# An attention and SwiGLU kernel: ScalarE's instructions in one up phase keep the order in which the program writes them

## The chip, the cores and the metric

The kernel runs on one core of a Trainium2 chip. Such a core has a matrix engine (TensorE, PE in the profile), a vector engine (VectorE, DVE), a scalar engine (ScalarE, ACT) and a general engine (GpSimd, POOL), each with an instruction stream of its own. They read and write an on-chip memory of 128 partitions (SBUF); TensorE writes its results to a second one (PSUM), from which VectorE and ScalarE take them. Transfers to and from the chip's large memory, and here also between two places of SBUF, are issued from the queue of SyncE (SP) or of ScalarE. An engine takes up its instructions in the order of its stream; between engines, semaphores hold an instruction back until what it needs is there.

The metric is the device time of one execution in microseconds (us), the median of several. Lower is better.

## The reference

```python
def _attn_ref(q, k, v, g_norm):                      # q, k, v: (8, 8, 576, 64)
    kv = np.einsum('bhsd,bhse->bhde', k, v)
    out = np.einsum('bhsd,bhde->bhse', q, kv)
    rms = np.sqrt(np.mean(out * out, axis=-1, keepdims=True) + 1e-06)
    return (out / rms * g_norm).astype(np.float32)

def _moe_ref(x, w_gate, w_val, w_out):               # (4608, 512), (512, 1536) twice, (1536, 512)
    g = x @ w_gate
    silu = g * (1.0 / (1.0 + np.exp(-g)))
    val = x @ w_val
    return (silu * val @ w_out).astype(np.float32)
```

The first function is attention without a softmax: for each of 8 batches and 8 heads k-transposed times v gives a 64 x 64 matrix, q times that matrix gives the output, and each row of 64 is divided by its root mean square and multiplied by `g_norm`. The result, brought into the shape 4608 x 512, is the `x` of the second function, a feed-forward block with a SiLU gate. Inputs and outputs are float32 (the weights of the second function arrive as 64-bit words, which the kernel turns into float32 itself).

## The kernel before, in words

The 4608 rows are cut into nine blocks of 512. For each block there is an attention part (class `Att`), which makes the transposed activations `x`, and a feed-forward part (class `Ffn`), which has an up phase (the products with `w_gate` and `w_val`) and a down phase (the product with `w_out`). The large products are made by Strassen's scheme in Winograd's form: seven products of half-size matrices in place of eight, numbered 1 to 7, with sums of operands before them and sums of results after them. Blocks 0, 1 and 2 go alone (function `alone`), blocks 3 to 8 in pairs with two levels of the scheme. While block n computes, the attention part of later blocks is done between its steps.

**The up phase of block 2.** Method `Ffn.up` goes through six units, numbered 0 to 5 (class `Up`, one per 256 columns of the weights). The sequence of a unit's products is line 701: products 1 and 5 of this unit, 4 and 3 of the unit before, then 6, 2 and 7 of this one. After the last unit, `last.end()` (lines 733 to 737) makes its products 3 and 4. What is done with each product's result, by the unit's methods:

- after product 1, line 677: ScalarE copies bank `b` from PSUM to the tile piece `s`; after product 6, line 681: it copies bank `b` to `u2`; after product 7, line 711: it copies bank `b` to `u3`, and line 714 applies SiLU to `s`.
- after product 4, line 724: ScalarE applies SiLU to bank `b`, and line 725 has GpSimd multiply the result with `u3` into the hidden activations `h`.
- after product 2, line 707: VectorE adds bank `a` to `s`; after product 7, line 715: it adds bank `c` to `u3`; after product 3, line 728: it adds bank `c` to `u2`, and line 729 has GpSimd multiply it with `s` into `h`.
- The bank `b` runs on through products 1, 6, 7 and 4, so each of these waits for the copy after the one before it. The bank `c` runs on through products 5 and 3: product 3 of a unit accumulates onto `c`, and so waits for the VectorE add of line 715, which reads `c` after product 7.
- `h_sums` (lines 1080 to 1086) makes two VectorE sums for each unit, the owed ones of the unit before after line 715.

All simple VectorE and GpSimd operations are made through the helpers of lines 130 to 132, so the profile puts every add on line 130, every subtraction on line 131 and every multiplication on line 132; tile names tell them apart. The matmuls of the up and down phases are all on line 661.

**The attention work that is woven in.** Function `ahead` (lines 1253 to 1295) gives the up phase of block 2 a table of extra steps, keyed by unit and product. The keys that matter: at (4, 1) `place_x` (line 515) issues 16 transfers inside SBUF, line 522, all on SyncE's queue here, which bring the transposed activations of block 3 to their place in `arena`; at (4, 2) `raw` adds transfers that send weight pieces to memory (line 920); at (5, 5) `gain_x` (line 526) has ScalarE multiply these activations by `g_norm`, two instructions of 128 x 1024 elements on line 529, which need all 16 transfers; at (5, 6) `sums` appends the four VectorE sums of `sum_steps` (lines 536 to 542), which are then issued two at a time after the next products: s1 and s3 after product 2 of unit 5, the other two after product 7.

**What sets the order.** The kernel is written with a library that schedules: each engine's stream is arranged at build time by priority and by the scheduler's own estimate of when an instruction can start, and it may differ from the order in which the program writes the instructions. Two means bind it: `tc.issue_after(i)` puts what a block writes behind one instruction, and the context manager `in_order` (lines 135 to 150) ties each instruction written inside it to the one written before it on the same engine. It takes the engines as arguments. Around block 2, TensorE is in order as a whole (line 1366), and VectorE during the up phase (line 1341). ScalarE, GpSimd and SyncE are not. In the kernel before, the scheduler has put the two instructions of line 529 behind line 714 of unit 5, that is, behind the last SiLU that precedes the end of the up phase.

Of the kernel before, what the change touches and what calls it, by code (L numbers as in the profile page):

```python
# [18 lines left out]
def kernel(  # L19
# [41 lines left out]
    nc = tc.nc  # L61
# [72 lines left out]
    @contextmanager  # L134
    def in_order(*engines):

        traced = nc.cur_bb.bb.instructions
        last = traced[-1]
        yield
        start = next(k for k in reversed(range(len(traced))) if traced[k] is last) + 1  # L140
        before = {}
        for i in traced[start:]:
            if engines and i.engine not in engines:
                continue
            if i.engine in before:
                tc.add_manual_dep(
                    i, before[i.engine].name,
                    mybir.DependencyInfo(mybir.DependencyClass.NoSync, mybir.DependencyReason.DATA), reason="order",
                )
            before[i.engine] = i  # L150
# [1074 lines left out]
    def weights(upto):  # L1225
        nonlocal rounded
        while rounded < min(upto, len(pieces)):
            load_weights(rounded + 4)
            round_w(*pieces[rounded])
            rounded += 1  # L1230

    def t2(place, b22, b11):

        sub(nc.vector, place, b22, place)
        add(nc.vector, place, place, b11)
# [9 lines left out]
    def visit(ffn, att, gs, apart=False):  # L1245

        with tc.issue_after(ffn.multiplied.ins):
            for g in gs:
                att.kv(g, apart)
        if att.n < B:  # L1250
            ffn.visited = att.positions

    def ahead(ffn, att, then):

        def load(att, i):
            return lambda: ffn.sends.extend(att.quarter_steps(i, (0, 1), (nc.sync,)))

        def first():
            visit(ffn, att, (0, 1))
            ffn.sends += [load(att, 0), lambda: then.load_kv(0), load(att, 1)]  # L1260

        def turn(i):
            ffn.chores.append(lambda: att.turn_q(i))

        def second():
            visit(ffn, then, (0,), True)
            ffn.sends.append(lambda: then.load_kv(1))

        def half(i):
            with tc.issue_after(ffn.multiplied.ins):  # L1270
                att.heads(i, range(NS), (m_psum, m_psum))
            ffn.visited = att.multiplied
            ffn.chores += att.chores(i)
            if i:
                ffn.chores += att.turn_steps()

        def rest():
            for i in range(2):
                load(then, i)()

        def raw():
            for j in range(2, NP):
                ffn.sends += raw_steps(j)

        def sums():
            ffn.chores.extend(att.sum_steps())

        for j in (NP - 2, NP - 1):
            ffn.making.extend(kept_steps(j, chunks(h_alone[:, NF - 4 :]) if j == NP - 1 else chunks(xi_alone)))

        return {
            (0, 1): first, (1, 6): lambda: turn(0), (1, 7): second, (2, 1): lambda: half(0), (2, 6): lambda: turn(1),
            (2, 7): rest, (3, 1): lambda: half(1), (3, 7): lambda: visit(ffn, then, (1,), True), (4, 1): att.place_x,
            (4, 2): raw, (5, 5): att.gain_x, (5, 6): sums,
        }

    def alone(n):
        ffn = Ffn(n, blocks[n])
        nxt = blocks[n + 1]
        if n == 0:  # L1300

            with tc.issue_after(squared.ins), tc.issue_after(scaled.ins):
                weights(2)
            ffn.plain_up(0, (0,))
            copied = blocks[0].copied
            blocks[0].turn_x(1)
            for f in range(NF):
                with tc.issue_after(blocks[0].copied.ins if f else copied.ins):
                    weights(2 * (f + 2))
                ffn.plain_up(f) if f else ffn.plain_up(0, (1,))  # L1310
            weights(len(pieces))
            pairs = wo.rearrange("p (j e) d -> p e j d", e=2)
            t2(pairs[:, 0, :, HD:DM], pairs[:, 1, :, HD:DM], pairs[:, 0, :, 0:HD])
            nxt.room = xi_alone.rearrange("p a b c -> p (a b c)")

            with tc.issue_after(sent.ins):
                for i in range(2):
                    nxt.load_kv(i)
                for i in range(2):
                    nxt.load_q(i)  # L1320
            ffn.plain_end()
            for g in range(2):
                nxt.kv(g)
            nxt.turn()
        elif n == 1:

            def third():
                visit(ffn, nxt, (0,))
                nxt.load_kv(1)

            def two_thirds():
                visit(ffn, nxt, (1,))
                for i in range(2):
                    nxt.load_q(i)

            ffn.up({(1, 7): third, (3, 7): two_thirds})
            nxt.turn()
            for g in range(2):
                blocks[PAIRED].load_kv(g)
        else:  # L1340
            with in_order(nc.vector.engine):
                ffn.up(ahead(ffn, nxt, blocks[PAIRED + 1]))
            nxt = blocks[PAIRED + 1]
            nxt.turn()
            for g in range(2):
                blocks[PAIRED + 2].load_kv(g)
        if n == 2:
            ffn.down_.opens = PAIRED

        def inner_sums():  # L1350
            with tc.issue_after(nxt.scaled.ins):
                blocks[PAIRED].inner_sums()

        ffn.down(nxt, {7: inner_sums} if n == 2 else {})
        if n == 0:
            blocks[2].load_kv(0)

            with tc.issue_after(nxt.halves[0].ins):
                for j in range(NP // 2):
                    t2(wv[j][:, 0:2], wv[j][:, 2:4], wg[j][:, 0:2])  # L1360
            with tc.issue_after(ffn.down_.s4.ins):
                for j in range(NP // 2, NP):
                    t2(wv[j][:, 0:2], wv[j][:, 2:4], wg[j][:, 0:2])

    for n in range(PAIRED):
        with in_order(nc.tensor.engine) if n == 2 else ExitStack():
            alone(n)
# [61 lines left out]
```

## Time and profile before

| | us |
|---|---|
| median of three executions | 1023.85 (1022.38 to 1024.58) |
| the profiled execution's own time | 1026.13 |
| its span, first to last instruction | 1024.4 |
| TensorE busy with matmuls | 998.7 (97% of the span) |
| VectorE busy | 667.3 (65%) |
| ScalarE busy | 232.1 (23%) |
| GpSimd busy | 369.8 (36%) |

The profile comes from one execution. Its time lies 1.73 us above its span and 2.28 us above the median. Times inside it are counted from the span's start. A row of the timeline gives start, duration, engine, line, operation, output and inputs, and in brackets how long the engine had stood idle and what ended that. A matmul's end is modelled, so its duration overlaps that of the next one; the distance between starts is the pace. The up phase of block 2 ends, and its down phase begins, at about 361 us.

### The profile page before, as it was taken

Reading aid. Unit: us, or ns where it says so; the run is one execution under the profiler, and the core shown is the slowest. Engines: PE = TensorE matmul, PEld = TensorE weight load, DVE = VectorE, ACT = ScalarE, POOL = GpSimd, SP = SyncE. Lnnn points to the kernel's source line nnn. Section 1 sums busy time; section 2 is a strip of 40 time slices with the busy share of each in tenths; the row PEclk is TensorE's granted clock in tenths of the full one; section 3 lists DMA queues with packets and bytes.
Section 4 is the critical chain, followed back from the end, with each engine's and each line's share of the span. In section 5 each row is a group of like instructions: output and inputs, shape, how many; then the busy total and the mean of one; then the engine's idle time right before and its main releaser. Section 6 shows DMA issues by size and latency. Waiting matters only on the chain.

```text
span 1024.4 us, 17093 instructions
## 1 busy us (share of the span) xinstructions
PE 998.7 (97%) x6506; PEld 832.7 (81%) x6506; DVE 667.3 (65%) x1118; ACT 232.1 (23%) x367; POOL 369.8 (36%) x290
## 2 busy tenths in 40 slices
PE   5999999999999799999999999999999999999998
PEld 4544688888888688888888888888888888888887
DVE  2998897759767475666666846666767566666211
ACT  2765111221122212121111212112112121121100
POOL 0000363525444140454556003554650026546600
PEclk9999999999999899999999999999999999999999
DMA  7689643656566925676753265667321655553011
GB/s 218 200 266 251 118 88 134 217 165 147 165 140 113 227 58 162 167 208 164 169 144 51 89 159 152 160 173 179 101 34 50 144 160 146 150 145 95 1 42 42
DMA packets 254290, 143.23 MB, mean 140 GB/s; under 512 B 149504, under 2 KB 236544, under 8 KB 254208
## 3 DMA queue, kind: packets, MB, share of 16 engines
q1 hardware_dynamic: 223488, 138.20, 50.2%
q10 hardware_dynamic: 30656, 3.94, 2.4%
q8 instruction: 52, 0.85, 0.4%
q14 instruction: 30, 0.25, 0.1%
q0 software_dynamic: 64, 0.00, 0.0%
HBM read 104.99 MB, written 28.70 MB: 131 GB/s over the span
## 4 chain that ended last, share of the span: by engine, by line
PE 76%; DVE 9%; DMA 5%; SPq 5%; issue 2%; ACT 2%; POOL 1%; DVEq 0%; POOLq 0%; ACTq 0%
PE b L811 21%; PE b L661 21%; PE c L661 11%; PE c L811 10%; PE a L661 5%; PE a L811 5%; SPq L333 2%; DVE r L190 1%; PE m L431 1%; DMA ld<-in_moe_w_out_dram 1%; DVE arena L131 1%; PE m L370 1%; DVE arena L199 1%; SPq L522 1%; DMA ld<-in_v_dram 1%
## 5 line engine op out<-in xcount | busy, mean ns | idle before, releaser
L811 PE MATMUL b<-arena,t 128*128 128x256 f32 x1008 | 244.6, 381 | 0.0
L811 PEld LDWEIGHTS b<-arena,t 128*128 128x128 f32 x1008 | 189.9, 190 | 29.9 <-DVE r L130 2.8
L130 POOL TENSOR_TENSOR r<-r 128x256 f32<-128x256 f32 (+1 forms) x90 | 94.8, 1054 | 246.2 <-DMA t<-w 149.5
L130 DVE TENSOR_TENSOR r<-b,r 128x512 f32<-128x512 f32 (+1 forms) x234 | 139.0, 607 | 61.1 <-PE b L811 56.0
L130 DVE TENSOR_TENSOR r<-c,r 128x512 f32<-128x512 f32 (+1 forms) x170 | 104.7, 624 | 108.6 <-PE c L811 41.1
L131 POOL TENSOR_TENSOR t<-wo 128x512 f32<-128x512 f32 x54 | 78.1, 1468 | 175.9 <-DVE wo L130 107.2
L132 POOL TENSOR_TENSOR arena<-r 128x1024 f32<-128x1024 f32 (+1 forms) x54 | 100.9, 1883 | 112.3 <-DVE r L130 84.4
L130 DVE TENSOR_TENSOR r<-a,r 128x512 f32<-128x512 f32 x93 | 59.2, 637 | 110.5 <-PE a L661 73.6
L811 PE MATMUL c<-arena,t 128*128 128x256 f32 x504 | 122.5, 379 | 1.0 <-ACT r L825 0.8
L131 DVE TENSOR_TENSOR arena<-arena 128x512 f32<-128x512 f32 (+3 forms) x96 | 104.3, 1102 | 18.1 <-PE b L661 14.0
L811 PEld LDWEIGHTS c<-arena,t 128*128 128x128 f32 x504 | 95.6, 190 | 14.7 <-ACT r L825 1.2
L661 PE MATMUL b<-wo,arena 128*128 128x256 f32 x432 | 98.3, 382 | 0.4 <-issue 0.3
L661 PE MATMUL b<-t,arena 128*128 128x256 f32 x432 | 96.4, 379 | 1.4 <-POOL s L130 0.7
L661 PEld LDWEIGHTS b<-t,arena 128*128 128x128 f32 x432 | 81.9, 190 | 13.2 <-POOL s L130 1.1
L661 PEld LDWEIGHTS b<-wo,arena 128*128 128x128 f32 x432 | 81.2, 190 | 12.7 <-DVE arena L132 0.9
L825 ACT COPY r<-b 128x512 f32<-128x512 f32 x54 | 31.6, 585 | 191.2 <-PE b L811 191.2
L131 POOL TENSOR_TENSOR t<-arena 128x512 f32<-128x512 f32 x36 | 51.4, 1438 | 59.5 <-DMA w<-t 23.3
L811 PE MATMUL a<-arena,t 128*128 128x256 f32 x252 | 66.1, 379 | 0.0
L811 PEld LDWEIGHTS a<-arena,t 128*128 128x128 f32 x252 | 47.9, 190 | 6.5
L661 PE MATMUL c<-wo,arena 128*128 128x256 f32 x216 | 48.2, 379 | 0.2 <-DVE r L130 0.2
L661 PE MATMUL c<-t,s 128*128 128x256 f32 x216 | 48.1, 379 | 0.0
L661 PE MATMUL a<-wo,arena 128*128 128x256 f32 x216 | 48.1, 379 | 0.0
(105 smaller groups left out, 1228.5 us busy)
## 6 DMA issues: line engine op xcount, KB each, us to landing
t<-w SPq DMA_DIRECT2D x180, 256.0 KB, 3.1
out_dram<-r SPq DMA_DIRECT2D x17, 512.0 KB, 2.9
ld<-in_k_dram SPq DMA_DIRECT2D x26, 288.0 KB, 4.8
ld<-in_v_dram SPq DMA_DIRECT2D x26, 288.0 KB, 5.9
t<-w SPq DMA_DIRECT2D x54, 128.0 KB, 2.4
ld<-in_moe_w_gate_dram SPq DMA_DIRECT2D x12, 512.0 KB, 4.7
ld<-in_moe_w_val_dram SPq DMA_DIRECT2D x12, 512.0 KB, 4.6
ld<-in_moe_w_out_dram SPq DMA_DIRECT2D x12, 512.0 KB, 5.5
```

The lines of the kernel that those rows point to most:

```text
L130: add = lambda e, o, a, b: e.tensor_tensor(out=o, in0=a, in1=b, op=OP.add)
L131: sub = lambda e, o, a, b: e.tensor_tensor(out=o, in0=a, in1=b, op=OP.subtract)
L132: mul = lambda e, o, a, b: e.tensor_tensor(out=o, in0=a, in1=b, op=OP.mult)
L190: return nc.vector.scalar_tensor_tensor(out=mag, in0=mag, scalar=3, in1=sign, op0=OP.logical_shift_left, op1=OP.bitwise_xor)
L199: return nc.vector.tensor_tensor(out=dst.bitcast(U32), in0=self.mag.rearrange("p (a b) -> p a b", a=a, b=b), in1=unit.bitcast(U32).rearran ...
L333: queue.dma_start(out=to[32 * r : 32 * (r + 1), j, g0:g1], in_=q[b, 4 * i + 2 * j + h, s0 : s0 + 32 * (g1 - g0), 32 * d : 32 * (d + 1)].re ...
L370: self.positions = nc.tensor.matmul(self.kv_ps[r][u * D : (u + 1) * D, g, :], lhsT=k[:, u, c, :], rhs=v[:, u, c, :], start=(c == 0), stop= ...
L431: self.multiplied = nc.tensor.matmul(self.ps[i][u][p : p + D, t, j, :], lhsT=self.qt[rows, tile_t, head, p : p + D], rhs=kvs[b % 3][rows, ...
L522: placed = queue.dma_start(out=dst[rows[b], :, rows[a]], in_=src[rows[a], :, rows[b]])
L661: self.ffn.multiplied = nc.tensor.matmul(banks[e][:, e], lhsT=lhsT, rhs=rhs, start=first and i == 0 and (e == 0 or banks[0] is not banks[1 ...
L811: self.ffn.multiplied = nc.tensor.matmul(ps[:, i], lhsT=stream.use(self.ffn.n, self.j, o, p), rhs=self.operand(o, p), start=first and i == ...
L825: nc.scalar.copy(out=dst, in_=ps)
```

## The change

In the up phase of block 2, `in_order` is now given ScalarE beside VectorE: ScalarE's instructions of that phase are tied to each other in the order in which the program writes them.

```diff
         else:
-            with in_order(nc.vector.engine):
+            with in_order(nc.vector.engine, nc.scalar.engine):
                 ffn.up(ahead(ffn, nxt, blocks[PAIRED + 1]))
             nxt = blocks[PAIRED + 1]
             nxt.turn()
```

In the built program this moves the two instructions of line 529 forward past four others of ScalarE's stream. The order around them, before and after (the unit in brackets):

```
before: L677 (5), L724 (4), L681 (5), L711 (5), L714 (5), L529, L529, L724 (5), L677 (down phase)
after:  L677 (5), L529, L529, L724 (4), L681 (5), L711 (5), L714 (5), L724 (5), L677 (down phase)
```

On GpSimd the two multiplications of unit 4 change places: line 729 now comes before line 725. The streams of TensorE, VectorE and SyncE hold the same instructions in the same order.

## The prediction

> **What bounds the kernel now.** I read the page first. TensorE is busy almost all of the span. Its busy time and its granted clock both dip once in mid-kernel, in the same slice, the fourteenth of forty (25.6 us each, so 333 to 359 us):
>
> ```profile
> PE   5999999999999799999999999999999999999998
> ...
> PEclk9999999999999899999999999999999999999999
> ```
>
> There block 2's up phase ends. Next, what TensorE waited for over the whole span:
>
> ```profile
> PE c L661 <- DVE r L130: 5.9, 3, 5.2
> ...
> PE m L431 <- DVE r L386: 1.5, 2, 1.2
> ```
>
> One wait of 5.2 us for a VectorE add is the longest of the kernel. The chain that ended last, in order of time, shows who made that add late:
>
> ```profile
> 347.99 2.76 DMA w<-arena
> 350.75 0.62 ACT r L714
> 351.37 2.08 ACT arena L529 x2
> 353.45 0.02 issue
> 353.48 0.69 DVE arena L130
> 354.17 0.60 DVE arena L131
> 354.77 0.61 DVE r L130
> 355.38 0.04 issue
> 355.43 3.78 PE c L661 x8
> ```
>
> Read from below: product 3 of unit 5 (PE c) waits for the add of line 715 (DVE r L130, at 354.69 in VectorE's timeline); that add stands in VectorE's fixed order behind the sums s1 and s3 (DVE arena), and s1 waits for the two gain instructions (L529). VectorE's timeline says the same of its idle time:
>
> ```profile
> 348.60 0.69 DVE L130 TENSOR_TENSOR r<-a,r 128x512 f32<-128x512 f32 x1 [2.83 <-PE a L661]
> 353.48 0.69 DVE L130 TENSOR_TENSOR arena<-arena 128x512 f32<-128x512 f32 x1 [4.18 <-ACT arena L529]
> ```
>
> ScalarE's timeline shows where the gains stand, and how idle ScalarE is before them:
>
> ```profile
> 339.98 0.58 ACT L677 COPY r<-b 128x512 f32<-128x512 f32 x1 [0.69 <-PE b L661]
> 343.35 0.60 ACT L724 ACTIVATE r<-b 128x512 f32<-128x512 f32 x1 [2.79 <-PE b L661]
> 346.81 0.58 ACT L681 COPY r<-b 128x512 f32<-128x512 f32 x1 [2.86 <-PE b L661]
> 350.26 0.58 ACT L711 COPY r<-b 128x512 f32<-128x512 f32 x1 [2.87 <-PE b L661]
> 350.74 0.63 ACT L714 ACTIVATE r<-r 128x512 f32<-128x512 f32 x1
> 351.27 2.17 ACT L529 ACTIVATE arena<-arena,gain 128x1024 f32<-128x1024 f32 x2
> ```
>
> Last, busy time and clock in short stretches (the value after POOL's count is the granted clock):
>
> ```profile
> 350.20:352.00 1.80, 0.02 (x1) 0.00 (x0) 0.00 (x0) 1.74 (x3) 0.00 (x0) 1.00 1.03 261
> 353.40:355.40 2.00, 0.00 (x0) 0.00 (x0) 1.92 (x4) 0.04 (x1) 0.00 (x0) 0.50 1.04 257
> 359.00:360.20 1.20, 1.20 (x4) 1.00 (x3) 0.69 (x1) 0.00 (x0) 0.13 (x1) 0.50 1.01 225
> 360.20:361.30 1.10, 1.10 (x6) 0.94 (x5) 0.00 (x0) 0.00 (x0) 1.10 (x1) 0.99 0.30 62
> ```
>
> TensorE stops at 350.22, its clock halves at 353.4 and is whole again at 360.2. So the stall costs twice: in idle time, and in products 3 and 4 at half speed.
>
> [...] it fell 3.2 us after the stop and rose 4.8 us after the restart at 355.43. [...] line 715's add, with its input long copied (line 711 ended at 350.84), sat behind s1 until 354.69. [...]
>
> **The change part by part.** Only line 529's pair moves on ScalarE, from behind L714 to behind the L677 of 339.98. It issues no DMA.
>
> *When can the gains run?* In the built program they wait for eight transfer counts, each that of the second group of eight placing transfers (656 on each count); the weight sends behind them carry 672 and 688. The placing transfers are issued on SyncE's queue from 328.55 to 339.30 (16, 0.67 apart, the last at 338.67), and the trace has 2.1 to 2.4 us from issue to landing. Landing is then at 340.9, or, if counted from the end of the issue (0.63 later), 341.6. L677 ends at 340.56, so ScalarE waits at most about a microsecond, and the two gains (2.17) end between 343.1 and 343.8.
>
> *Who is queued behind them?* L724 of unit 4 (wants 343.35), L681 (346.81), L711 (350.26), L714. The first is at most 0.45 late. Its result feeds line 725 on GpSimd, which now stands behind line 729: 729 at 345.85 as before, 725 from about 347.1 to 348.4, in place of 344.03 to 345.30. Its readers are the owed sums (355.29 before, about 351.5 now) and the down phase (358 at the earliest): nothing. L681 and L711 keep their times, as L724 is out of the way by 344.4. Cost of the move: 0. Without this cover it would be the full 2.17.
>
> *What follows on VectorE?* After line 707 (348.60 to 349.29), s1 and s3 run at once at 0.60 each, to about 350.7. Line 715 then waits for L711. In unit 4 that pair stood at 338.17 and 338.79, 0.62 apart; so 350.26 + 0.62 = 350.88. From line 715 to TensorE's restart took 355.43 - 354.69 = 0.74; restart at 351.62. Idle: 351.62 - 350.22 = 1.40, where it was 5.21: saved **3.81**.
>
> *The clock.* A stall of 1.40 is well under the 3.2 after which it fell here. TensorE's wait of 1.17 before 123.56 (L386) left the clock at 1.00 in the stretches around it. Products 3 and 4 then take 1.73 each plus 0.10 for the restart (1.83 in block 1, 232.25 to 234.08): 3.56. Before, from 355.43 to the first matmul of the down phase at 361.34: 5.91. Saved **2.35**. The down phase starts at 351.62 + 3.56 = 355.18.
>
> *Is that start free otherwise?* It needs h of unit 5 only in its last matmuls: line 728 may be 0.6 late behind the remaining sums (VectorE busy to about 354.1 with the owed pair and these two), GpSimd's line 729 then ends near 356.0, and unit 5's matmuls come at 355.18 + 20 x 0.216 = 359.5. Free.
>
> *Does the shift survive?* By the first down product's end (366.68 before) VectorE stood idle 2.32 for TensorE, ScalarE 4.66 for it, GpSimd follows VectorE's h sums, and SyncE's queue from there to 460 waits mostly for TensorE's releases (23.1, 22.2, 7.1 and 4.6 us, against 5 for transfers). From 355 to 400 the chain is TensorE without a gap. All later work is paced by TensorE, so it moves as one.
>
> Sum: -3.81 - 2.35 = **-6.2 us**. Against the profiled execution: span 1024.4 to 1018.2, own time 1026.13 to 1019.9. That execution lies 2.28 above the median shown; taking the difference to the median, 1023.85 - 6.2 = **1017.7 us**.
>
> **The rivals.** *The clock halves all the same.* Then only 3.81 is saved: 1020.0. For it: [...] one fall is all there is. Against: the stall at 123 us.
>
> *The gain is lost later.* A transfer with a time of its own would hold the pair of blocks 3 and 4. For it: near 441 TensorE waits 0.3 us for streamed weights (t<-w), so that stream has no slack, and eight k and v loads issued 348.75 to 354.1 keep their times. Against: those loads have landed by about 361 (6.7 us or less after issue), and the stream's first issue comes at 375.9, waiting for TensorE. Then 1023.9.
>
> *The wait moves forward and grows (the slower side).* The chain names a weight send that lands at 350.75 as what came last before L714. If the gains in fact waited for it, they would now hold L724, L681 and all of product 7 back. This decides from a landing of 344.1 on (2.15 + 0.5 + 0.1 before L681's 346.81), and turns to a loss from about 349. With 350.75: gains to 352.95, L681 to 354.05, product 7 from 354.1 at half clock to 357.6, L711 and line 715 to 359.0, product 3 at 359.05; down phase at 362.6 if the clock is back, 365.0 if not, against 361.34: +1.2 to +3.7, in the middle 1026.3. Against: the waits of the built program name the placing transfers alone, and L714 waits for VectorE's count, not for a transfer.
>
> That the change does nothing is excluded: the built streams differ.
>
> **How the numbers follow.** Forecast 0.86, clock 0.06, lost later 0.04, slower 0.04. The forecast's unknowns are the restart (0.2), the landing (0 to 0.45 that should not matter), and the runs' own scatter of about 1.1 either way; I take 1016.1 to 1019.2 for it, and extend the range upward to the clock's case: 1016.0 to 1020.4. A difference of 0.2% (2.05 us) is about what these runs can tell from none. The first two cases are faster: with a little off for scatter 0.91; same 0.05, slower 0.04.
>
> **What would show it.** Line 529 at 340.9 to 341.7, with idle time ended by the placing transfers; s1 at about 349.3; TensorE's wait for the VectorE add 1.4 us; the clock without a dip at 353; the down phase at 355.2 and L811's first matmul near 393.8 instead of 399.98. L681 later than 346.9 would speak for the slower rival, the dip for the clock's, a new TensorE wait after 360 for the loss. The forecast is wrong if the landing is later than 344.1.

## The result, and the profile after

| | before | after |
|---|---|---|
| median of five executions each, us | 1023.85 (1022.38 to 1025.31) | 1018.16 (1017.20 to 1020.08) |
| ratio | | 0.9946, 95% interval 0.9932 to 0.9960 |
| span of the profiled execution, us | 1024.4 | 1016.4 |

The change makes the kernel faster by 5.7 us by the medians, 4.1 to 7.0 us by the interval of the ratio. The forecast was 6.2 us and 1017.7.

First the page of the changed kernel, TensorE's busy time and granted clock (in tenths of full speed, 9 for 90% or more) in forty slices:

```profile
PE   5999999999999999999999999999999999999998
...
PEclk9999999999999999999999999999999999999999
```

The dip in the fourteenth slice is gone from both rows. TensorE's waits over the span (total, times, longest):

```profile
PE c L661 <- DVE r L130: 2.1, 3, 1.4
...
PE c L811 <- DMA t<-w: 0.3, 1, 0.3
```

The 5.2 us wait is now 1.4 us, and the small wait for streamed weights near the paired blocks, 0.3 us before, has not grown. The chain that ended last, around the end of block 2's up phase:

```profile
348.63 0.59 ACT r L711
349.22 0.02 issue
349.25 0.70 DVE r L130
349.95 0.04 issue
349.99 1.99 PE c L661 x8
```

The gains (L529), the sums (DVE arena) and L714 have left the chain. What stays is what product 3 really needs: the copy of line 711 and the add of line 715. ScalarE's timeline shows where the gains went:

```profile
338.34 0.58 ACT L677 COPY r<-b 128x512 f32<-128x512 f32 x1 [0.69 <-PE b L661]
338.96 2.19 ACT L529 ACTIVATE arena<-arena,gain 128x1024 f32<-128x1024 f32 x2
341.72 0.60 ACT L724 ACTIVATE r<-b 128x512 f32<-128x512 f32 x1 [0.57 <-PE b L661]
345.17 0.58 ACT L681 COPY r<-b 128x512 f32<-128x512 f32 x1 [2.86 <-PE b L661]
348.63 0.58 ACT L711 COPY r<-b 128x512 f32<-128x512 f32 x1 [2.87 <-PE b L661]
```

They fill the idle time between L677 and L724; L724 still waits 0.57 us for TensorE after them and is not late. And VectorE's timeline:

```profile
346.97 0.69 DVE L130 TENSOR_TENSOR r<-a,r 128x512 f32<-128x512 f32 x1 [2.83 <-PE a L661]
347.58 0.68 DVE L130 TENSOR_TENSOR arena<-arena 128x512 f32<-128x512 f32 x1
348.18 0.68 DVE L131 TENSOR_TENSOR arena<-arena 128x512 f32<-128x512 f32 x1
349.25 0.69 DVE L130 TENSOR_TENSOR r<-c,r 128x512 f32<-128x512 f32 x1 [0.38 <-ACT r L711]
```

The sums s1 and s3 run without a wait, and line 715's add waits 0.38 us for the copy of L711, no longer for the gains.

Times of two executions can't be compared by their place in the span: up to L711 of unit 5 the profile after is already 1.63 us ahead (348.63 against 350.26). In the orders of the two streams the change reaches back no further than L677 of unit 5, 10.3 us ahead of that L711, and from there to L711 TensorE ran without a gap in both. In the profile before TensorE had waited 1.5 us for line 386 at about 123 us, and that wait is missing from the one after. Nor does the lead come from the change: in two more profiles of the unchanged kernel (below) that wait is missing too, and the same L711 starts at 348.77 and 347.99 us. So I measure from the start of L711 of unit 5:

| us from the start of L711 (unit 5) | before | after | difference |
|---|---|---|---|
| restart of TensorE (product 3) | 5.17 | 1.36 | 3.81 |
| first matmul of the down phase | 11.08 | 4.92 | 6.16 |
| first matmul of the paired blocks (L811) | 49.56 | 43.40 | 6.16 |
| end of the span | 674.1 | 667.8 | 6.4 |

What was won at the end of the up phase arrives whole at the pair and at the end of the span.

### The profile page after: what moved, and what is told of

The parts are those of the page before. It is cut to its first block, busy times and chain, and to the rows that moved or that the text cites. A ratio compares the mean times of both kernels' runs of the same rounds, so it can differ in the third digit from the quotient of the medians.

```text
span 1016.4 us, 17091 instructions
## 1 busy us (share of the span) xinstructions
PE 995.9 (98%) x6506; PEld 831.0 (82%) x6506; DVE 665.9 (66%) x1118; ACT 232.5 (23%) x367; POOL 368.3 (36%) x290
## 4 chain that ended last, share of the span: by engine, by line
PE 81%; DVE 8%; DMA 5%; ACT 1%; issue 1%; POOL 1%; SPq 1%; DVEq 0%; POOLq 0%; ACTq 0%
PE b L661 23%; PE b L811 21%; PE c L661 12%; PE c L811 10%; PE a L661 6%; PE a L811 5%; DMA ld<-in_moe_w_out_dram 2%; PE m L431 1%; PE m L370 1%; DVE r L190 1%; DVE arena L131 1%; DVE arena L199 1%; DMA arena<-in_v_dram 1%; SPq L333 1%; POOL t L131 1%
## 5 line engine op out<-in xcount | busy, mean ns | idle before, releaser
L811 PE MATMUL b<-arena,t 128*128 128x256 f32 x1008 | 244.5, 381 | 0.0
L811 PEld LDWEIGHTS b<-arena,t 128*128 128x128 f32 x1008 | 190.0, 190 | 29.6 <-DVE r L130 2.4
L811 PE MATMUL c<-arena,t 128*128 128x256 f32 x504 | 122.5, 379 | 1.0 <-ACT r L825 0.8
L811 PEld LDWEIGHTS c<-arena,t 128*128 128x128 f32 x504 | 95.6, 190 | 14.7 <-ACT r L825 1.2
L811 PE MATMUL a<-arena,t 128*128 128x256 f32 x252 | 66.1, 379 | 0.0
L811 PEld LDWEIGHTS a<-arena,t 128*128 128x128 f32 x252 | 47.9, 190 | 6.5
```

The source lines that it names most:

```text
L811: self.ffn.multiplied = nc.tensor.matmul(ps[:, i], lhsT=stream.use(self.ffn.n, self.j, o, p), rhs=self.operand(o, p), start=first and i == ...
```

## The experiments

The theory: the loss was one TensorE stall, because line 715's add stood in VectorE's fixed order behind sums that waited for the gains (its copy was done at 350.84, it began at 354.69); it cost idle time and, on top, half clock. Rivals: the early place of the gains brings something itself (the exchange on GpSimd among it); the gains' new place has a price that is merely covered here; the clock term is not what the prediction took it for. "Distance" below is from the start of L711 of unit 5 to the first matmul of the down phase: 11.08 us in the first profile of before, 4.92 in that of the changed kernel. Each diff is against the changed kernel. The times of before differ a little from group to group, as each group of runs has its own.

**The gains late, the sums out of the way.** ScalarE's stream around L711 is that of before, with the gains behind L714; VectorE's four sums now come behind line 715's add.

```diff
-            (4, 2): raw, (5, 5): att.gain_x, (5, 6): sums,
+            (4, 2): raw, (5, 7): lambda: (att.gain_x(), att.sums()),
```

> ScalarE's stream is that of the kernel before (the two gains behind L714); instead VectorE's four sums are written behind line 715's add. If the cost of before was that line 715's add stood behind sums that wait for the gains, the wait is gone here too: L715 about 0.62 us after L711's start, TensorE idle 1.4 us, down phase 4.9 us after L711's start (11.08 before), about 6 us faster than before, as the changed kernel. If it is the gains' early place itself that brings the time (the exchange on GpSimd, or ScalarE's order later on), this one stays at the time of before.

Measured: 1018.64 us against 1024.35, ratio 0.9947 (0.9930 to 0.9963). ScalarE's, VectorE's and TensorE's timelines of this run, a line or two of each:

```profile
349.36 0.59 ACT L711 COPY r<-b 128x512 f32<-128x512 f32 x1 [2.87 <-PE b L661]
...
350.37 2.17 ACT L529 ACTIVATE arena<-arena,gain 128x1024 f32<-128x1024 f32 x2
```

```profile
349.97 0.69 DVE L130 TENSOR_TENSOR r<-c,r 128x512 f32<-128x512 f32 x1 [1.58 <-ACT r L711]
...
352.57 0.69 DVE L130 TENSOR_TENSOR arena<-arena 128x512 f32<-128x512 f32 x1 [1.05 <-DMA ld<-in_v_dram]
```

```profile
350.72 1.99 PE L661 MATMUL c<-arena 128*128 128x256 f32 x8 [1.40 <-DVE r L130]
```

The gains are as late as they were, and nothing is lost: line 715's add comes 0.61 us after L711, TensorE waits 1.40 us, the distance is 4.92. So the late gains were harmless in themselves; their harm came through the place of the sums ahead of line 715's add. (The profile names a load as what ended VectorE's wait for s1 at 352.57; s1 waits for the gains, which end at 352.54.)

**The gains in a third place.** Between L681 and L711; GpSimd's two multiplications then keep the order of before.

```diff
-            (4, 2): raw, (5, 5): att.gain_x, (5, 6): sums,
+            (4, 2): raw, (5, 6): lambda: (att.gain_x(), sums()),
```

> As the changed kernel, but the gains stand behind L681 and just ahead of L711 (so L724 of unit 4 is as early as before, and GpSimd's two multiplications keep the order of before). Theory: only the place ahead of L711 counts; the gains end about 2.7 us after L681's start, 0.7 us before L711 can begin, so the same time as the changed kernel (within 0.3 us), TensorE idle 1.4 to 1.6 us. Rival (the early landing and the order on GpSimd matter): slower than the changed kernel by 1 us or more.

Measured: 1017.96 us, ratio 0.9938 (0.9923 to 0.9953), distance 4.92. ScalarE's and TensorE's timelines:

```profile
344.81 0.59 ACT L681 COPY r<-b 128x512 f32<-128x512 f32 x1 [2.86 <-PE b L661]
345.29 2.19 ACT L529 ACTIVATE arena<-arena,gain 128x1024 f32<-128x1024 f32 x2
348.26 0.59 ACT L711 COPY r<-b 128x512 f32<-128x512 f32 x1 [0.78 <-PE b L661]
```

```profile
349.62 1.99 PE L661 MATMUL c<-arena 128*128 128x256 f32 x8 [1.40 <-DVE r L130]
```

With GpSimd's order as before and the gains 6.7 us later than in the changed kernel relative to L711 (2.97 us ahead of it in place of 9.67), the stall is the same 1.40. Only the place ahead of L711 counts; the exchange on GpSimd brings and costs nothing.

**The stall rebuilt.** The changed kernel, with the sum s1 written again so many times ahead of line 715's add. With N repeats:

```diff
-            ffn.chores.extend(att.sum_steps())
+            s1, s3, *rest = att.sum_steps()
+            def slow():
+                s3()
+                for _ in range(N):
+                    s1()
+            ffn.chores.extend([s1, slow, *rest])
```

> The same with 7 repeats: TensorE idle 1.40 - 0.38 + 7 x 0.60 = 5.2 us, the stall of before rebuilt with the gains in their early place. If the whole loss of before is this stall, the time of before comes back: +3.8 us from idleness and up to +2.35 from the half clock over the changed kernel. If before lost time elsewhere too (the late gains as such), it stays 1 us or more below the time of before even where the clock halves.

> The changed kernel with the first sum repeated 4 times on VectorE ahead of line 715's add (same values written again), nothing else moved. TensorE idle 1.40 - 0.38 + 4 x 0.60 = 3.4 us instead of 1.40. If idle time and clock are two separate terms and the clock falls only after a stall of more than about 3.2 us, this costs about +2.0 us over the changed kernel with the clock whole, or up to +4.4 if the clock halves; the clock in the stretch after the stall tells which.

Measured: with seven 1025.28 us, ratio to before 1.0003 (0.9993 to 1.0014); with four 1022.23 us, ratio 0.9981 (0.9970 to 0.9993). A repeat took 0.70 us on average and not 0.60, so the stalls are 5.89 and 3.71 us. TensorE's timeline with seven:

```profile
355.97 3.78 PE L661 MATMUL c<-arena 128*128 128x256 f32 x8 [5.89 <-DVE r L130]
359.55 1.98 PE L661 MATMUL b<-arena,t 128*128 128x256 f32 x8
361.37 5.34 PE L661 MATMUL b<-wo,arena 128*128 128x256 f32 x24
```

A stall like that of before, made by VectorE alone while the gains run early, brings the time of before back. It came out 0.68 us longer than that of before (5.89 against 5.21), and the interval is about a microsecond wide on either side, so this excludes another loss of much more than a microsecond, not a smaller one. The distance is 11.24 with seven, 8.61 with four; over the changed kernel that is 6.32 and 3.69, of which 4.49 and 2.31 are idle time and 1.84 and 1.38 half clock. With four, the clock was expected whole or halved; it halved, for 3.41 us in the profile, and the mean granted clock of all 14 timed executions is 0.998 or less, where the changed kernel has 0.999 or 1.000.

Two shorter stalls followed:

> The changed kernel with the first sum repeated twice ahead of line 715's add. A repeat took 0.70 us in the runs with 4 and 7, so TensorE idle 1.40 - 0.38 + 2 x 0.70 = 2.4 us. Theory (the clock falls only after a stall of more than about 3.2 us): clock whole, +1.0 us over the changed kernel, 1.0 us in the distance from L711 to the down phase. Rival (it can fall after a shorter stall): half speed in product 3, +1.5 us or more on top.

> The changed kernel with the first sum repeated once ahead of line 715's add: TensorE idle about 1.7 us, [...]. [...] the clock stays whole and the distance from L711 to the down phase is 5.2 us (4.92 in the changed kernel); [...] it falls [...] and the distance is 6.2 to 7.0.

Two repeats: 1018.95 us, ratio 0.9948 (0.9930 to 0.9967) over four executions; one repeat (a single execution): 1017.1 us beside 1023.2 for before. TensorE's timeline with two repeats, and its busy time and clock in stretches (the clock stands third from the end):

```profile
350.78 3.48 PE L661 MATMUL c<-arena 128*128 128x256 f32 x8 [2.25 <-DVE r L130]
354.06 2.13 PE L661 MATMUL b<-arena,t 128*128 128x256 f32 x8
356.03 1.24 PE L661 MATMUL b<-wo,arena 128*128 128x256 f32 x5
```

```profile
348.60:350.70 2.10, 0.00 (x0) 0.00 (x0) 2.07 (x5) 1.08 (x2) 0.00 (x0) 1.00 1.06 239
351.20:354.50 3.30, 3.30 (x10) 2.55 (x9) 1.81 (x4) 0.00 (x0) 0.00 (x0) 0.50 1.05 221
354.60:356.00 1.40, 1.40 (x8) 1.25 (x7) 0.39 (x1) 0.00 (x0) 0.88 (x1) 1.00 1.06 227
```

Here the expectation missed, and the rival held: in the profiled execution the clock halved after a stall of only 2.25 us, and TensorE was already at work again when it did (from 350.78 on; the clock is 1.00 in the stretch up to 351.10, 0.50 in that from 351.20). It seems not to halve every time: of the four timed executions, which the profiled one is among, two have a mean granted clock of 0.998 over the whole execution (1020.63 and 1018.64 us) and two of 1.000 (1019.26 and 1016.78). With one repeat (stall 1.53, distance 5.05) the clock stayed whole, the first of the two outcomes on record; the stall came out shorter than the 1.7 us that the run was to test.

**How far the cover reaches.** The changed kernel with four, then eight more ScalarE passes right behind the gains, which multiply the same activations by 1.0.

```diff
+        def gain():
+            att.gain_x()
+            for i in range(N):
+                x = att.x[:, 2 * (i % 2) : 2 * (i % 2) + 2].rearrange("p o k t -> p (o k t)")
+                nc.scalar.activation(out=x, in_=x, func=ACT.Copy, scale=1.0)
...
-            (4, 2): raw, (5, 5): att.gain_x, (5, 6): sums,
+            (4, 2): raw, (5, 5): gain, (5, 6): sums,
```

> The changed kernel with four more ScalarE passes of 128 x 1024 behind the gains (multiplication by 1.0, same values). Gains and passes end 0.62 + 6 x 1.09 = 7.2 us after L677's start; L724 waits for them, L681 is 0.9 late, and product 7 has 0.95 us of slack for that. Theory (the gains' cover reaches to about L681): 0 to 0.2 us over the changed kernel. Rival (L724 or GpSimd's multiplication of unit 4 is on the path): the full 4.4 us.

> The same with eight passes: the cover is used up. Gains and passes end 11.5 us after L677's start, L681 at 12.0, product 7 at 12.65 in place of 8.36: a new TensorE stall of 4.3 us, long enough to halve the clock. This is the slower rival of the prediction built on purpose: +4.3 us from idleness and 1.4 to 2.35 from the clock over the changed kernel, 5.7 to 6.6 together, about the time of the kernel before.

Measured: with four 1018.12 us, ratio 0.9938 (0.9919 to 0.9957); with eight 1023.16 us, ratio 0.9994 (0.9982 to 1.0005). ScalarE's timeline with four:

```profile
339.74 2.19 ACT L529 ACTIVATE arena<-arena,gain 128x1024 f32<-128x1024 f32 x2 [0.81 <-DMA arena<-r]
341.84 3.88 ACT L1285 ACTIVATE arena<-arena 128x1024 f32<-128x1024 f32 x4
345.62 0.57 ACT L724 ACTIVATE r<-b 128x512 f32<-128x512 f32 x1
346.10 0.57 ACT L681 COPY r<-b 128x512 f32<-128x512 f32 x1
```

L724 is 3.9 us late against the changed kernel, counted from L677, and L681 0.9 us; from L677 to the down phase it takes 15.39 us instead of 15.21. In this execution the gains also waited 0.81 us for the last placing transfer, so the landing is close to L677's end and not always ahead of it. TensorE's timeline with eight:

```profile
349.16 2.61 PE L661 MATMUL b<-arena,t 128*128 128x256 f32 x8 [2.82 <-ACT r L681]
353.17 3.78 PE L661 MATMUL c<-arena 128*128 128x256 f32 x8 [1.40 <-DVE r L130]
356.74 2.10 PE L661 MATMUL b<-arena,t 128*128 128x256 f32 x8
358.68 5.34 PE L661 MATMUL b<-wo,arena 128*128 128x256 f32 x24
```

The cover is used up: product 7 now waits 2.82 us for L681 (a pass took 0.96 us, not 1.09, so less than the 4.3 expected), the clock halves for 6.83 us, and the way from L677 to the down phase grows from 15.21 to 20.86. So a ScalarE held up long enough does stall product 7, as the forecast's slower rival had it; the eight passes, 7.67 us together, take back about the whole gain and no more. A late transfer ahead of the gains was not tried.

**The kernel before, two more profiles.**

> The kernel before once more, for one more profile. [...] the stall of 5.21 us costs one or two windows of half clock, [...] distance from L711 to the down phase between 10.0 and 11.1 us (11.08 in the first profile), [...]. If the fall follows 3.2 us after the stop, as the prediction has it, the distance is 11.08 again.

> The same once more: another execution, [...]. Either the distance from L711 to the down phase differs from 11.08 [...], or it is 11.08.

Measured: distances 10.25 and 10.41 us, where the first profile has 11.08; both lie within the expected 10.0 to 11.1, which was the author's estimate: its one or two windows stand for 3.41 and 6.83 us, the two lengths of half clock in the profiles until then. TensorE's timeline of the first of the two, and its clock in stretches:

```profile
353.94 3.52 PE L661 MATMUL c<-arena 128*128 128x256 f32 x8 [5.21 <-DVE r L130]
357.30 1.89 PE L661 MATMUL b<-arena,t 128*128 128x256 f32 x8
359.02 5.34 PE L661 MATMUL b<-wo,arena 128*128 128x256 f32 x24
```

```profile
350.30:353.60 3.30, 0.00 (x0) 0.00 (x0) 1.61 (x3) 1.66 (x2) 0.00 (x0) 1.00 1.01 251
353.70:357.00 3.30, 3.06 (x7) 2.52 (x8) 2.24 (x5) 0.00 (x0) 0.00 (x0) 0.50 1.05 224
357.10:359.00 1.90, 1.90 (x10) 1.69 (x9) 0.69 (x1) 0.00 (x0) 0.68 (x1) 1.00 1.05 223
```

The clock falls 4.92 and 5.41 us after TensorE's stop in these two and 3.18 us in the first, so there is no fixed time from the stop to the fall. The stall is 5.21 us in all three, the half clock is not the same: it lasts 6.83 us in the first profile and 3.41 us in these. The clock term is 11.08, 10.25 and 10.41, each less 4.92 and 3.81: 2.35, 1.52 and 1.68 us.

**Product 4 ahead of product 3.** A version that takes part of the remaining 1.40 us, for block 2's last unit:

```diff
-            for p in (3, 4):
+            for p in (4, 3) if self.ffn.n == 2 else (3, 4):
```

> The changed kernel with the last unit's product 4 ahead of product 3 (block 2 alone). Product 4 needs only L711's copy, product 3 line 715's add, which is done while product 4 runs. TensorE idle 0.66 us instead of 1.40: 0.75 us saved in the distance from L711 to the down phase, about 0.7 us faster than the changed kernel, which is near what the timing can tell. If line 728 or 729 is then late for the down phase's last matmuls, a new wait there takes some of it back.

Measured: 1017.29 us against 1024.65, ratio 0.9932 (0.9918 to 0.9946). TensorE's timeline:

```profile
347.64 1.97 PE L661 MATMUL b<-arena,t 128*128 128x256 f32 x8 [0.77 <-ACT r L711]
349.44 1.89 PE L661 MATMUL c<-arena 128*128 128x256 f32 x8
351.17 5.34 PE L661 MATMUL b<-wo,arena 128*128 128x256 f32 x24
```

The distance is 4.26 us, 0.66 less than in the changed kernel, and no TensorE wait for lines 728 or 729 has come up. The intervals of the two ratios overlap, so the timing alone doesn't tell this version from the changed kernel; the profile does.

## Why the prediction was right, point by point

- **The cause.** Right, and shown from two sides: taking the sums out of line 715's way removes the loss with the gains left late, and delaying line 715 alone brings it back.
- **The landing and the cover.** The gains began 0.62 us after L677's start, as soon as it was done; the prediction had 0.9 to 1.7, with a wait for the placing transfers as its sign. That sign is not in the changed kernel's profile, but in those of the four passes (0.81 us of wait, 1.39 after L677's start) and of product 4 first (0.42 us, 1.01). Its limit, that nothing is lost until the gains end about when L681 wants to start, held: with passes that delayed L681 by 0.9 us the cost was 0.18 us.
- **Idle time.** 1.40 us forecast and measured, 3.81 saved.
- **The start of the down phase.** Forecast 355.18 - 350.26 = 4.92 us after L711, measured 4.92.
- **The late line 728, GpSimd's exchange.** Line 728's add began at 352.02, right behind the remaining sums, and GpSimd made both multiplications of unit 4 one after the other from 344.27 to 346.77; neither reached TensorE.
- **The shift survives.** Right: 6.16 us at the down phase, 6.16 at the pair, 6.4 at the end of the span.
- **The clock term.** Its 2.35 us was the loss of one execution, taken as if it were fixed. It is 2.35, 1.52 and 1.68 us in three profiles of before, so the saving is 6.16, 5.33 or 5.49 us. Which of these is usual, the mean granted clocks suggest. The two profiles with 3.41 us of half clock have 0.998, the first one with 6.83 us has 0.997. Of the 44 timed executions of before that were made beside the experiments with repeats, passes and moved gains, 9 have 0.998 and 35 have 0.997 or less; they take 1023.3 us on average at 0.998, 1024.4 at 0.997 and 1025.3 at 0.996. So the first profile was of the commoner kind, which was luck. The difference of the medians, 5.7 us with 4.1 to 7.0 as its interval, can't tell the three savings apart.
- **The reading behind it.** That a stall of 1.40 us leaves the clock whole came true, but "well under" 3.2 was a weaker argument than it sounded: 2.25 us was enough in one execution, and in the two later profiles of before the fall came 4.92 and 5.41 us after the stop. The 3.2 was the figure of one execution.
- **The rivals.** The clock did not fall in any of the profiles with a 1.40 us stall alone. One of the four timed executions with the gains in the third place has a mean clock of 0.998; no profile shows where the clock fell in it. No later loss came up. The gains did not wait for the weight send that the slower rival feared: they began as soon as L677 was done, and L681 started 6.83 us after L677's start, as before the change.

## What to carry to other kernels

An order that is fixed on one engine makes every instruction in it as late as the latest input ahead of it; if that input comes from an engine whose order is left to the scheduler, fix that one too, or put the dependent work behind what the bound engine waits for. In the kernel before, line 715's add began 3.85 us after the end of the copy that it needs, behind sums that waited for the gains. Before an instruction is moved forward, look at what stands behind it and when that is wanted: here the idle time ahead of L681 held 2.2 us of work at no cost, 3.9 us more cost 0.18, and 7.7 us more spent the gain. And a stall that borders on half clock should be priced as a range from several profiles, not from one: the same stall of 5.21 us cost 1.52, 1.68 and 2.35 us by the half clock in three profiles.

## What the runs showed of the hardware

The stall at the end of block 2's up phase, the half clock that came with it in the same profile, and the mean granted clock of that execution:

| run | stall, us | half clock in mid-kernel, us | mean granted clock |
|---|---|---|---|
| product 4 first | 0.77 | none | 0.999 |
| the changed kernel | 1.40 | none | 0.999 |
| gains late / third place / four passes | 1.40 | none | 1.000 |
| one repeat | 1.53 | none | 1.000 |
| two repeats | 2.25 | 3.41 | 0.998 |
| eight passes | 2.82, then 1.40 | 6.83 | 0.997 |
| four repeats | 3.71 | 3.41 | 0.998 |
| before, second profile | 5.21 | 3.41 | 0.998 |
| before, third profile | 5.21 | 3.41 | 0.998 |
| before, first profile | 5.21 | 6.83 | 0.997 |
| seven repeats | 5.89 | 6.83 | 0.997 |

In the changed kernel the clock falls only at about 1015.3 us, behind the last matmul, which makes its mean 0.999.

In these profiles stalls of 0.77 to 1.53 us left the clock whole, and those of 2.25 to 5.89 us came with half clock. The stall alone does not tell how much: one of 5.21 us came with 3.41 us of it in two executions and with 6.83 in a third, and the fall came 3.18, 4.92 or 5.41 us after the stop. Nor does it always tell whether: with two repeats two of the four timed executions have a mean clock of 1.000, and with eight passes one of the twelve, the fastest (1020.84 us). Of those three executions there is no profile, so how long their stalls were is not shown. Why executions of one kernel differ in this is not shown either. The lengths of the stalls rest on modelled ends of matmuls.
